# Soft-capped attention, gated MLP and gated convolution on one core: earlier loads of weight pieces and last values, and a third key tile added on VectorE for six head pairs

## The chip, the cores and the metric

The kernel runs on one core of one Trainium2 chip, in a single launch. The metric is the device time of that core in microseconds (us). The kernel before takes 324.7 us, the median of three runs (323.39, 324.70 and 325.33). One execution was profiled; it took 323.47 us, of which 321.3 us lie between its first and its last instruction.

## The reference, cut to what matters

Three stages run one after the other on 2 batches of 448 positions. The change touches the first alone.

```python
# 1. attention, 2 batches x 12 heads, 448 positions, head size 64
scores = (q @ k.T) / sqrt(64)
scores = cap * tanh(scores / cap)               # cap = 30
attn = softmax(scores)                          # exp, divided by (sum over keys + 1e-9)
x = concat_heads(attn @ v)                      # (2, 448, 768)
# 2. gated MLP, d_model 768, d_ff 1024
h = gelu(x @ w_in); u, v = halves of h
x = x + (u * (w_sg @ layernorm(v) * g_ln + b_sg)) @ w_out
# 3. gated convolution over the positions, three taps
h = relu(x @ w_in2); y = (h * sigmoid(conv(h))) @ w_out2
```

What the change computes otherwise is the sum over keys in the softmax: the terms are added in another place, and the sum is the same.

## The kernel before, in words

**Pairs, halves and rounds.** The 24 heads are worked in 12 pairs, numbered 0 to 11. The 448 keys of a head are cut in tiles of 128, 128, 128 and 64. A pair has two halves: half 0 holds the first two key tiles of both heads, half 1 the third tile and the last 64 keys. The loop in `attention` counts rounds R; in round R = 2N + half the function `scores` issues the products of queries and keys of pair N for that half. ScalarE applies tanh and exp to them in turn (`soft`, `expo`), and leaves exp(scores) in a tile `raw`. The scores of a half go to one PSUM tile `sc` that has one buffer, so the next half's scores wait until the tanh of this half has read it. I call rounds 2N and 2N+1 together "the stretch of pair N".

**Values and sums.** Two rounds later (`LAGS`), `values` multiplies exp(scores) by the values V into PSUM: half 0 first (key tiles 0 and 1), then half 1 (the last 64 keys, from the tile `vlast`, and key tile 2). So in the stretch of pair N TensorE issues the scores of pair N and the values of pair N-1. The sum over keys is taken by products with tiles of ones, in sets of four matmuls of 32 columns each. For half 0 VectorE first adds key tile 1 to key tile 0 (line 462; the result is `held[N]`, a tile named `sm`), and one set multiplies `sm` by ones. In half 1 one set multiplies key tile 2 of `raw` by ones and one set the last 64 keys. All TensorE instructions of this stage are chained in the order in which the code is written (`ordered`), so one that waits holds up all behind it.

**Normalising.** When a pair is done, ScalarE copies output and sums to `E` (line 532); a DMA from GpSimd's queue gathers the sums of two pairs into `ss` (line 534), VectorE takes the reciprocal (lines 552 and 553), a DMA writes it to `d` (line 556), four DMAs spread it over the partitions as `rb` (line 562), and VectorE multiplies (line 569) and splits the result in a high and a low part, `X`.

**Loads.** SyncE issues nearly all DMAs of this stage, and `sync` chains them in one order. `load(N+2)`, in round 2N, brings queries and keys (`qr`: two DMAs, `kr`: three); `load_v(N+1)` brings V; `load_vlast(n0, n1)` brings the last values of pairs n0 to n1-1 in four DMAs: pairs 0 to 2 at the start, pairs 3 to 11 in round 6. `prep_q` and `prep_k` split queries and keys on VectorE (lines 106 and 109) before the scores of that pair.

**Weight pieces.** The 12 pieces of the MLP's first weight, 512 KB each and stored as 64-bit numbers, are loaded into tiles `f` (named `f64` in the program; four buffers) in the rounds that the table `WIN` lists, and decoded in three steps that fall due 5, 6 and 7 ticks later; a round has two ticks. A decode is a cast to `hd` on VectorE (line 155; for later pieces on ScalarE, line 153), a shift-and-or (line 159), a cast to `WI` (line 165) and a subtraction (line 168). The first step is pinned behind the newest instructions noted in `lasta` and `lastv`:

```python
            with pin(lasta), pin(lastv):
                if top_eng == "a":
                    A.activation(half, top, AF.Copy)
                else:
                    V.tensor_copy(half, top)
```

The scheduler of the language sets the rest of VectorE's order by a simulated time, within such pins.

**Filling and the rest.** In rounds 15, 19 and 23 (`FILL`) TensorE also does six matmuls of the MLP; they need `X` and the first weight pieces. From about 108 us on the MLP and the convolution follow, with TensorE working without a gap. Lines 112 to 114 are their matmuls.

Of the kernel before, what the change touches and what calls it, by code (L numbers as in the profile page):

```python
# [23 lines left out]
NK = DM // P  # L24
# [13 lines left out]

TAKEN = 4

WARM = 10

K0 = 2 * P

IDLE = {0: (1, 4)}

WIN = (3, 5, 7, 9, 12, 15, 17, 19, 21, 22, 23, 24)
WOS = (0, 0, 1, 4, 4, 7, 7, 7, 10, 10, 11, 15)
W2I = (12, 12, 13, 13, 15, 17, 22, 24, 26, 30, 30, 33)
W2O = (0, 0, 1, 3, 4, 6, 7, 8, 8, 10, 10, 11, 11, 11, 11, 12, 13, 14, 15, 17, 18, 18, 19, 19)  # L50
# [3 lines left out]
def stages(  # L54
# [160 lines left out]
    def wi_piece(src, h, k):  # L215
        return WI[h], src, k, h * DH, (h + 1) * DH
# [66 lines left out]
    def attention(att, psa):  # L283
# [58 lines left out]
                for c in range(2):  # L342
                    sync(vlast[c * D : (c + 1) * D, n0:n1, r], v[r, n0:n1, 3, r])

        load_vlast(0, 3)
        if WARM:

            wz = att.tile([P, S], F32R, tag="rb", name="wz", bufs=2)
# [37 lines left out]
        def scores(N, half, then=None):  # L386

            R = 2 * N + half
            q, K = Qt[N], Kt[N % 2]
            ps = psa.tile([P, 4, 512], F32, tag="sc", name="sc", bufs=1)  # L390
            raw = raws[N, half] = att.tile([P, 4, S], F32, tag="raw", name="raw", bufs=3)

            sc = qreg if N else qscale

            def soft(x, ps):
                with pin(lasta):
                    lasta[0] = A.activation(x, ps, AF.Tanh, scale=sc)  # L397
                if N == 1 and half:
                    with pin(lasta):
                        late.pop()()  # L400
                if half or N:
                    expo(x)

            def expo(x):
                with pin(lasta):
                    lasta[0] = A.activation(x, x, AF.Exp, scale=creg)  # L406

            if half:
                ps = ps.rearrange("p (h a) c -> p h (a c)", h=2)[:, :, : 3 * 288]
                ps = ps.rearrange("p h (i c) -> p h i c", i=3)[:, :, :, :HS]  # L410
                raw = raws[N, half] = raw[:, :3].rearrange("p t s -> p (t s)").rearrange(
                    "p (h i c) -> p h i c", h=2, i=3
                )

            for g in range(2 * half, 2 * half + 2):
                to = ps
                if R == 0 and g == 0:
                    to = sums.rearrange("p (t c) -> p t c", t=3)
                c = slice(g * P, (g + 1) * P)
                if g < 2:  # L420

                    for i, (j, l) in enumerate(((0, 0), (0, 1), (1, 0))):
                        for h in range(2):
                            r = slice(h * D, (h + 1) * D)
                            ordered(to[:, g * 2 + h, :S], lhsT=K[r, j, c], rhs=q[r, l], start=i == 0, stop=i == 2)
                elif g == 2:
                    qr, kr = qraw[N]
                    x = qr.rearrange("p (i c) -> p i c", i=2)
                    for h in range(2):
                        r = slice(h * D, (h + 1) * D)  # L430
                        for i in range(2):
                            o, w = slice(i * D, (i + 1) * D), slice(K0 + i * D, K0 + (i + 1) * D)
                            ordered(ps[o, h, :2], lhsT=kr[r, w], rhs=x[r], start=True, stop=True)
                else:

                    qr, kr = qraw.pop(N)
                    for h in range(2):
                        r = slice(h * D, (h + 1) * D)
                        for i in range(2):
                            ordered(  # L440
                                ps[i * D : (i + 1) * D, h, 2], lhsT=kr[r, ST:],
                                rhs=qr[r, i * HS : (i + 1) * HS], start=True, stop=True,
                            )
                if N == 0 and g < 2:
                    soft(raw[:, 2 * g : 2 * g + 2], to[:, 2 * g : 2 * g + 2, :S])
                    if g:
                        expo(raw[:, 0:2])
                        expo(raw[:, 2:4])
                if R == 2 and g == 0:
                    set_guard()  # L450
                if R in IDLE and g == IDLE[R][0]:
                    for _ in range(IDLE[R][1]):
                        ordered(idle, lhsT=wz[:, :P], rhs=wz, start=True, stop=True)
            if then:
                then()
            if half:
                soft(raw, ps)
            elif N:
                soft(raw, ps[:, :, :S])
            if half == 0:  # L460
                held[N] = att.tile([P, 2, S], F32, tag="sm", name="sm", bufs=2)
                sms[N] = [V.tensor_tensor(out=held[N], in0=raw[:, 0:2], in1=raw[:, 2:4], op=ALU.add)]  # L462
# [27 lines left out]
        def values(N, half, done=False):  # L490
            if not done:
                if half == 0:
                    start_values(N)
                    value(N, 0)
                    value(N, 1)
                else:
                    value(N, 3)
                    value(N, 2)
            ps, su, both = acc[N]
            raw = raws.pop((N, half))  # L500

            for g in range(2 * half, 3 * half + 1):
                x = raw if half else held.pop(N)
                for t in range(4):
                    h, c = divmod(t, 2)
                    ordered(
                        su[t * 32 : (t + 1) * 32],
                        lhsT=ones[2 if g < 3 else c],
                        rhs=x[:, h, g - 2 + c if g == 2 else 2] if half else x[:, h, c * HS : (c + 1) * HS],
                        start=False, stop=g == 3, tile_position=(0, t * 32), skip_group_check=True,  # L510
                    )
            if half:
                del acc[N]
                norm(N, both)
# [94 lines left out]
        for R in range(2 * NN + LAGS[1] + 1):  # L609
            N, half = divmod(R, 2)  # L610
            if R == 23:
                columns(att)
            for j, at in enumerate(WIN):
                if at == R:
                    top_eng = "v" if R < 11 else "a"
                    wdec(*wi_piece(w_in, j // NK, j % NK), att, 4, hi_eng="v", wait=(5, 6, 7), top_eng=top_eng)
            if R < 2 * NN:
                if half == 0 and N + 2 < NN:
                    load(N + 2)
                if half == 0 and N + 1 < NN:  # L620
                    load_v(N + 1)
                if R == 6:
                    load_vlast(3, NN)
                if R == 1:

                    start_values(0)
                    scores(N, half)
                    value(0, 0)
                    value(0, 1)
                elif R == 3:  # L630

                    def sums0():
                        values(0, 1, True)
                        for _ in range(2):
                            ordered(idle, lhsT=wz[:, :P], rhs=wz, start=True, stop=True)

                    scores(N, half, sums0)
                    done += 1
                else:
                    scores(N, half)  # L640
                if R == 2:
                    values(0, 0, True)
                    value(0, 3)
                    value(0, 2)
                    done += 1
                if half == 0 and N + 1 < NN:
                    with pin(sms[N - 1]) if N else ExitStack():
                        prep_q(N + 1)
                        prep_k(N + 1)
            def units():  # L650

                i, k0, k1 = FILL[R]
                if k0 == 0:
                    if i == 1:
                        fill[-1] = psa.tile([P, 4, 512], F32, tag="sc", name="fi", bufs=1)
                    fill[i] = fill[-1][:, i, :S] if i % 2 else psm.tile([P, 512], F32, tag="mo", name="mo")[:, :S]
                for k in range(k0, k1):
                    mmw(fill[i], 0, i, k, ordered)
                if k1 == NK:
                    u_done(0, i, fill[i])  # L660
            if R in FILL and R >= 2 * NN:
                units()
            tick()
            if R > 2 and done < 2 * NN and R - done >= LAGS[R >= LAGS[2]]:
                values(*divmod(done, 2))
                done += 1
                if R == 2 * NN:
                    values(*divmod(done, 2))
                    done += 1
            if R in FILL and R < 2 * NN:  # L670
                units()
            tick()
# [428 lines left out]
```

## Time and profile before

| | |
|---|---|
| runs shown | 323.39, 324.70, 325.33 us; median 324.7 |
| profiled execution | 323.47 us, span 321.3 us |
| TensorE (PE) busy | 313.5 us, 98% of the span |
| VectorE (DVE) busy | 222.0 us, 69% |
| ScalarE (ACT) busy | 206.6 us, 64% |
| GpSimd (POOL) busy | 37.4 us, 12% |
| mean granted TensorE clock | 0.997 of full speed |
| DMA moved | 37.73 MB, 117 GB/s over the span |

Times in rows are us from the span's start. PE rows are matmuls and PEld rows weight loads, which run beside them; a 32-bit matmul that isn't in the fp32r form shows as two records, so a set of four with ones is eight records. In a timeline a row is one group of like instructions: its start, its length, engine, line, operation, what is written from what, the count, and in brackets how long the engine had been idle and what ended that. In a table of stretches the numbers behind the busy times (with counts of instructions) are the granted TensorE clock, the DMA share and GB/s. SPq is SyncE's queue: its time is that of issuing, not of moving data.

### The profile page before, as it was taken

What the parts mean: (1) busy time and instruction counts of PE and PEld (TensorE: products, weight loads), DVE (VectorE), ACT (ScalarE), POOL (GpSimd) and SP (SyncE); (2) the same over time, 40 slices, a digit from 0 to 9 for tenths busy, and PEclk for the clock granted to TensorE, in tenths of its full rate; (3) what the DMA queues carried; (4) which work ended last, traced back from release to release, by engine and by line L of the source; (5) the groups of instructions that cost most, each with busy time, mean ns of one, the idle gap of its engine ahead of it and who ended that gap; (6) DMA issues with size and microseconds to landing.
All of it is one profiled execution on the core that took longest, in us unless ns stands there. A gap on an engine that the chain in (4) does not pass through costs nothing.

```text
span 321.3 us, 6377 instructions
## 1 busy us (share of the span) xinstructions
PE 313.5 (98%) x2398; PEld 259.3 (81%) x2398; DVE 222.0 (69%) x460; ACT 206.6 (64%) x342; POOL 37.4 (12%) x75
## 2 busy tenths in 40 slices
PE   8999999999999999999999999999999999999993
PEld 6566656666677889988999999999999999999992
DVE  3458596698568879988996899979999998000000
ACT  4999989898973447746944754568886988111010
POOL 3000141441333020211112000000000000000000
PEclk9999999999999999999999999999999999999998
DMA  3478886857242153331134670021583201110111
GB/s 114 116 219 209 246 232 151 240 165 243 93 131 89 31 159 97 93 98 50 51 98 134 203 285 1 3 65 66 141 317 98 74 27 58 58 60 29 57 57 39
DMA packets 24528, 37.73 MB, mean 117 GB/s; under 512 B 7609, under 2 KB 22473, under 8 KB 24489
## 3 DMA queue, kind: packets, MB, share of 16 engines
q1 hardware_dynamic: 22552, 34.22, 35.1%
q0 software_dynamic: 1632, 2.61, 2.8%
q8 instruction: 21, 0.34, 0.5%
q10 hardware_dynamic: 304, 0.41, 0.4%
q14 instruction: 19, 0.15, 0.2%
HBM read 34.39 MB, written 2.79 MB: 116 GB/s over the span
## 4 chain that ended last, share of the span: by engine, by line
PE 81%; DMA 2%; DVE 0%; ACT 0%; SPq 0%; issue 0%; ACTq 0%
PE mo L113 18%; PE mo L112 18%; PE mo L114 18%; PE pv L380 8%; PE sc L380 4%; PE mo L795 3%; PE mo L797 3%; PE mo L796 3%; PE mo L380 3%; PE fi L380 2%; DMA ss<-E 1%; DMA kr<-in_kT_dram 1%; PE mo L841 1%; PE mo L842 1%; DVE sm L462 0%; ACT o L982 0%
## 5 line engine op out<-in xcount | busy, mean ns | idle before, releaser
L113 PE MATMUL mo<-X,WI 128*128 128x448 f32 x120 | 43.9, 366 | 0.0
L114 PE MATMUL mo<-X,WI 128*128 128x448 f32 x120 | 43.8, 365 | 0.0
L112 PE MATMUL mo<-X,WI 128*128 128x448 f32 x120 | 43.4, 365 | 0.0
L406 ACT ACTIVATE raw<-raw 128x1344 f32<-128x1344 f32 (+2 forms) x25 | 36.4, 1460 | 0.7
L397 ACT ACTIVATE raw<-sc 128x1792 f32<-128x1792 f32 (+1 forms) x22 | 32.4, 1474 | 4.4 <-PE sc L380 4.4
L112 PE MATMUL mo<-HG,W 128*128 128x448 f32 x96 | 34.4, 365 | 0.0
L114 PE MATMUL mo<-HG,W 128*128 128x448 f32 x96 | 34.4, 365 | 0.0
L113 PE MATMUL mo<-HG,W 128*128 128x448 f32 x96 | 34.4, 365 | 0.0
L380 PE MATMUL pv<-raw,V 128*32 128x224 f32 x576 | 32.9, 357 | 0.0
L985 ACT ACTIVATE o<-mo 128x448 f32<-128x448 f32 x11 | 5.8, 540 | 34.9 <-PE mo L114 31.7
L380 PEld LDWEIGHTS pv<-raw,V 128*32 128x32 f32 x576 | 19.0, 109 | 11.5 <-issue 5.6
L113 PEld LDWEIGHTS mo<-X,WI 128*128 128x128 f32 x120 | 22.5, 188 | 1.9
L114 PEld LDWEIGHTS mo<-X,WI 128*128 128x128 f32 x120 | 22.5, 188 | 1.9
L112 PEld LDWEIGHTS mo<-X,WI 128*128 128x128 f32 x120 | 22.5, 188 | 1.9
L153 ACT ACTIVATE hs<-f 128x256 f16<-128x256 bf16 x36 | 16.6, 488 | 7.8 <-DMA f<-in_w_in_dram 4.8
L114 PEld LDWEIGHTS mo<-HG,W 128*128 128x128 f32 x96 | 18.0, 188 | 1.4
L113 PEld LDWEIGHTS mo<-HG,W 128*128 128x128 f32 x96 | 18.0, 188 | 1.4
L112 PEld LDWEIGHTS mo<-HG,W 128*128 128x128 f32 x96 | 18.0, 188 | 1.4
L168 DVE TENSOR_TENSOR WI<-f,WI 128x256 fp32r<-128x256 f32 (+1 forms) x36 | 18.2, 509 | 1.0 <-ACT WI L163 0.7
L113 PE MATMUL mo<-gl,WO 128*128 128x448 f32 x48 | 17.4, 367 | 0.0
L114 PE MATMUL mo<-GH,WO 128*128 128x448 f32 x48 | 17.2, 366 | 0.0
L380 PE MATMUL sc<-Q,K 64*128 64x448 f32 x138 | 17.2, 380 | 0.0
(156 smaller groups left out, 683.9 us busy)
## 6 DMA issues: line engine op xcount, KB each, us to landing
f<-in_w_out_dram SPq DMA_DIRECT2D x36, 255.8 KB, 2.9
f<-in_w_in_dram SPq DMA_DIRECT2D x12, 511.8 KB, 5.7
f<-in_w_in_dram SPq DMA_DIRECT2D x24, 255.8 KB, 3.4
qr<-in_qT_dram SPq DMA_DIRECT2D x23, 112.0 KB, 4.0
rb<-d POOLq DMA_DIRECT2D x22, 112.0 KB, 3.4
out_dram<-o SPq DMA_DIRECT2D x11, 224.0 KB, 2.1
V<-in_vL_dram SPq DMA_DIRECT2D x12, 192.0 KB, 4.7
kr<-in_kT_dram SPq DMA_DIRECT2D x11, 112.0 KB, 4.9
```

The costliest lines, as they stand in the source:

```text
L112: matmul(ps, lhsT=whi, rhs=xhi, start=start, stop=False)
L113: matmul(ps, lhsT=whi, rhs=xlo, start=False, stop=False)
L114: matmul(ps, lhsT=wlo, rhs=xhi, start=False, stop=stop)
L153: A.activation(half, top, AF.Copy)
L168: V.tensor_tensor(out=lo, in0=f(low), in1=f(hi), op=ALU.subtract)
L380: lastm[0] = T.matmul(*args, **kw)
L397: lasta[0] = A.activation(x, ps, AF.Tanh, scale=sc)
L406: lasta[0] = A.activation(x, x, AF.Exp, scale=creg)
L795: T.matmul(ps, lhsT=xs(0, k), rhs=WI[1][:, 0, k], start=k == 0, stop=False)
L796: T.matmul(ps, lhsT=xs(0, k), rhs=WI[1][:, 1, k], start=False, stop=False)
L797: T.matmul(ps, lhsT=xs(1, k), rhs=WI[1][:, 0, k], start=False, stop=k == NK - 1)
L985: A.activation(o, ps, AF.Copy, scale=0.5)
```

## The change

It has three parts.

1. **The pieces are asked for sooner.** `WIN` moves the loads of the first nine pieces one or two rounds forward, and a new table `WAIT` makes up for it: the decode steps fall due as many ticks later, so each is written at the same tick as before.
2. **The last values come in four groups** of three pairs, in rounds 0, 4, 8 and 12 (`LAST`), instead of three pairs at the start and nine in round 6.
3. **In pairs 1, 2, 3, 5, 7 and 9 (`ADD`) VectorE also adds key tile 2 to the held sum.** The addition is noted in `lastv`, so later pinned instructions stand behind it. The set of products for half 0 goes, and the one that multiplied key tile 2 takes `held` instead. One set of four matmuls per pair is left out.

```diff
+ADD = (1, 2, 3, 5, 7, 9)
...
-WIN = (3, 5, 7, 9, 12, 15, 17, 19, 21, 22, 23, 24)
+WIN = (1, 3, 5, 7, 10, 13, 15, 17, 20, 22, 23, 24)
+
+WAIT = (9, 9, 9, 9, 9, 9, 9, 9, 7, 5, 5, 5)
+
+LAST = {0: (0, 3), 4: (3, 6), 8: (6, 9), 12: (9, 12)}
...
-        load_vlast(0, 3)
+        load_vlast(*LAST[0])
...
             if half:
                 soft(raw, ps)
+                if N in ADD:
+                    x = held[N].rearrange("p h (i c) -> p h i c", i=2)
+                    lastv[0] = V.tensor_tensor(out=x, in0=x, in1=raw[:, :, :2], op=ALU.add)
...
-            for g in range(2 * half, 3 * half + 1):
-                x = raw if half else held.pop(N)
+            for g in ((0, 3) if half else ()) if N in ADD else ((2, 3) if half else (0,)):
+                x = raw if g else held.pop(N)
...
-                        rhs=x[:, h, g - 2 + c if g == 2 else 2] if half else x[:, h, c * HS : (c + 1) * HS],
+                        rhs=x[:, h, c if g == 2 else 2] if g else x[:, h, c * HS : (c + 1) * HS],
...
-                    top_eng = "v" if R < 11 else "a"
-                    wdec(*wi_piece(w_in, j // NK, j % NK), att, 4, hi_eng="v", wait=(5, 6, 7), top_eng=top_eng)
+                    k, top_eng = WAIT[j], "v" if j < 4 else "a"
+                    wdec(
+                        *wi_piece(w_in, j // NK, j % NK), att, 4, hi_eng="v", wait=(k, k + 1, k + 2), top_eng=top_eng
+                    )
...
-                if R == 6:
-                    load_vlast(3, NN)
+                if R and R in LAST:
+                    load_vlast(*LAST[R])
```

**On TensorE**, in the stretch of pair 4, where the values of pair 3 are worked, before:

```order
L380 MATMUL sc_501<-Q_425,K0_87 128x448 x12
L380 MATMUL pv_157<-raw_408,V_311 32x224 x16
L380 MATMUL pv_157<-sm_423,ones2_144 32x224 x4
L380 MATMUL sc_557<-qr_304,kr_305 64x2x224 x4
L380 MATMUL sc_557<-qr_304,kr_305 64x224 x4
L380 MATMUL pv_157<-raw_456,vlast_108 64x224 x4
L380 MATMUL pv_157<-raw_456,V_311 32x224 x8
L380 MATMUL pv_157<-raw_456,ones2_144 32x224 x4
```

and now:

```order
L386 MATMUL sc_502<-Q_425,K0_87 128x448 x12
L386 MATMUL pv_157<-raw_408,V_314 32x224 x16
L386 MATMUL sc_552<-qr_307,kr_308 64x2x224 x4
L386 MATMUL sc_552<-qr_307,kr_308 64x224 x4
L386 MATMUL pv_157<-raw_452,vlast_108 64x224 x4
L386 MATMUL pv_157<-raw_452,V_314 32x224 x8
L386 MATMUL pv_157<-sm_423,ones2_144 32x224 x4
```

The set with `sm_423`, the held sum of pair 3, has moved behind the values of half 1, and the set with key tile 2 is gone.

**On VectorE**, from the split of pair 5's keys (`K1_88<-kr_395`) to the held sum of pair 4 (`sm_517`), before. `ss` are the sums of pairs 0 and 1, and `f64_453` is the third weight piece:

```order
L109 TENSOR_TENSOR K1_88<-kr_395,K1_88 128x256
L552 TENSOR_SCALAR ss_297<-ss_297,one_72 128x14
L155 CAST hd0_135<-f64_453 128x512
L553 RECIPROCAL ss_297<-ss_297 128x14
L159 SCALAR_TENSOR_TENSOR f64_453<-f64_453,hd0_135 128x512
L165 CAST WI0_76<-f64_453 128x512
L168 TENSOR_TENSOR WI0_76<-f64_453,WI0_76 128x512
L462 TENSOR_TENSOR sm_517<-raw_502 128x896
```

and now (`f64_278` is the second piece, `f64_359` the third, and `sm_518` the held sum of pair 4):

```order
L115 TENSOR_TENSOR K1_88<-kr_399,K1_88 128x256
L561 TENSOR_SCALAR ss_299<-ss_299,one_72 128x14
L161 CAST hd0_135<-f64_359 128x512
L562 RECIPROCAL ss_299<-ss_299 128x14
L165 SCALAR_TENSOR_TENSOR f64_359<-f64_359,hd0_135 128x512
L171 CAST WI0_76<-f64_359 128x512
L174 TENSOR_TENSOR WI0_76<-f64_359,WI0_76 128x512
L466 TENSOR_TENSOR sm_423<-sm_423,raw_452 128x896
L161 CAST hd1_136<-f64_278 128x512
L165 SCALAR_TENSOR_TENSOR f64_278<-f64_278,hd1_136 128x512
L171 CAST WI0_76<-f64_278 128x512
L471 TENSOR_TENSOR sm_518<-raw_503 128x896
```

The new addition for pair 3 stands behind the split of pair 5's keys, the sums of pairs 0 and 1 and a whole decode, and a second decode follows it ahead of pair 4's sum. (The last two rows have one subtraction into `WI0_76` between them, like the one shown.) Before, the second piece was decoded a pair earlier, in front of pair 3's sum.

**In SyncE's queue**, from V of pair 3 to the keys of pair 5, before (the names `qr_394` and `kr_395` are pair 5's):

```order
L86 DMA V_311<-in_vL_dram 128x384
L86 DMA f64_356<-in_w_in_dram 128x2047
L86 DMA qr_394<-in_qT_dram 64x448 x2
L86 DMA kr_395<-in_kT_dram 64x448
L86 DMA kr_395<-in_kT_dram 64x384
L86 DMA kr_395<-in_kT_dram 64x64
```

and now (`kr_399` is pair 5's):

```order
L92 DMA V_314<-in_vL_dram 128x384
L92 DMA vlast_108<-in_vL_dram 64x3x64 x4
L92 DMA f64_359<-in_w_in_dram 128x2047
L92 DMA qr_398<-in_qT_dram 64x448 x2
L92 DMA kr_399<-in_kT_dram 64x448
L92 DMA kr_399<-in_kT_dram 64x384
L92 DMA kr_399<-in_kT_dram 64x64
```

Four loads of last values have come in ahead of pair 5's queries and keys; the piece in this place is now the third instead of the second, which has moved up by a pair, as the first has.

## Rows read from the trace of the kernel before

**Rows 1.** The page: span, busy time and share of each engine.

```profile
span 321.3 us, 6377 instructions
...
PE 313.5 (98%) x2398; PEld 259.3 (81%) x2398; DVE 222.0 (69%) x460; ACT 206.6 (64%) x342; POOL 37.4 (12%) x75
```

**Rows 2.** Stretches of pairs 3, 4, 5, 7, and rest: length, PE, PEld, DVE, ACT, POOL busy.

```profile
24.53:31.37 6.84, 6.84 (x113) 4.40 (x109) 5.46 (x11) 6.62 (x6) 0.62 (x1) 1.00 0.92 222
31.37:38.22 6.85, 6.85 (x113) 4.39 (x110) 3.21 (x7) 6.62 (x6) 0.00 (x0) 1.00 0.87 214
38.22:45.78 7.56, 7.04 (x113) 4.19 (x110) 6.62 (x13) 6.58 (x6) 2.42 (x4) 1.00 0.86 255
...
52.61:61.35 8.74, 8.45 (x119) 5.26 (x115) 8.06 (x17) 8.48 (x8) 3.95 (x7) 1.00 0.79 208
...
108.20:316.00 207.80, 207.80 (x1008) 188.78 (x1006) 149.42 (x317) 116.89 (x259) 10.38 (x15) 1.00 0.29 93
```

**Rows 3.** Timeline of ScalarE in the stretch of pair 3.

```profile
26.06 1.66 ACT L397 ACTIVATE raw<-sc 128x1792 f32<-128x1792 f32 x1 [0.16 <-PE sc L380]
...
32.89 1.67 ACT L397 ACTIVATE raw<-sc 128x1792 f32<-128x1792 f32 x1 [0.17 <-PE sc L380]
```

**Rows 4.** Waits of TensorE's matmuls, those for VectorE's sums: total, times, longest.

```profile
PE pv L380 <- DVE sm L462: 0.8, 2, 0.5
```

**Rows 5.** Timeline of VectorE from 33 us on.

```profile
33.31 0.28 DVE L106 CAST K<-kr 128x256 fp32r<-128x256 f32 x1
...
34.38 0.23 DVE L552 TENSOR_SCALAR ss<-ss,one 128x14 f32<-128x14 f32 x1
38.44 0.47 DVE L155 CAST hd<-f 128x512 f16<-128x512 bf16 x1 [3.83 <-DMA f<-in_w_in_dram]
...
40.78 1.08 DVE L462 TENSOR_TENSOR sm<-raw 128x896 f32<-128x896 f32 x1
```

**Rows 6.** Timeline of VectorE before the held sum of pair 6.

```profile
51.70 0.23 DVE L552 TENSOR_SCALAR ss<-ss,one 128x14 f32<-128x14 f32 x1 [2.80 <-DMA ss<-E]
```

**Rows 7.** Timeline of TensorE in the stretch of pair 3.

```profile
25.96 1.76 PE L380 MATMUL pv<-raw,V 128*32 128x224 f32 x32
27.50 0.60 PE L380 MATMUL pv<-sm,ones 128*32 128x224 f32 x8
28.03 1.36 PE L380 MATMUL sc<-qr,kr 64*64 64x448 f32 x16
...
30.48 0.96 PE L380 MATMUL pv<-raw,ones 128*32 128x224 f32 x16
31.37 1.49 PE L380 MATMUL sc<-Q,K 64*128 64x448 f32 x12
```

**Rows 8.** Timeline of SyncE's queue: start and length of issuing.

```profile
7.73 2.62 SPq L86 DMA_DIRECT2D vlast<-in_vL_dram  x4
...
24.55 0.43 SPq L86 DMA_DIRECT2D f<-in_w_in_dram  x1
25.09 1.11 SPq L86 DMA_DIRECT2D qr<-in_qT_dram  x2
26.30 1.83 SPq L86 DMA_DIRECT2D kr<-in_kT_dram  x3
```

**Rows 9.** DMA issues from 15.2 to 16.4 us: count, KB each, us to landing.

```profile
qr<-in_qT_dram SPq DMA_DIRECT2D x2, 112.0 KB, 2.6
```

**Rows 10.** DMA issues between 26.3 and 28.2 us.

```profile
kr<-in_kT_dram SPq DMA_DIRECT2D x1, 96.0 KB, 4.6
```

**Rows 11.** Timeline of VectorE at the split of pair 3's keys.

```profile
19.74 0.29 DVE L106 CAST K<-kr 128x256 fp32r<-128x256 f32 x1 [0.86 <-DMA kr<-in_kT_dram]
```

**Rows 12.** Stretches at the end of the span: granted clock is the third number from the right.

```profile
318.00:319.00 1.00, 0.00 (x0) 0.00 (x0) 0.00 (x0) 0.00 (x0) 0.00 (x0) 1.00 0.33 112
...
320.00:321.40 1.40, 0.00 (x0) 0.00 (x0) 0.00 (x0) 0.00 (x0) 0.00 (x0) 0.50 0.02 6
```

**Rows 13.** DMA issues between 18.9 and 19.5 us.

```profile
f<-in_w_in_dram SPq DMA_DIRECT2D x1, 511.8 KB, 4.1
```

## The prediction

> **What bounds the kernel now.** I read the busy shares first. TensorE is busy for 98% of the span, VectorE for 69% and ScalarE for 64% [rows 1]. Then the same by stretch, because the shares are means over stages. From 108 us to 316 us TensorE is busy for all of 207.8 us [rows 2]: what happens before only moves this block, and a microsecond won or lost in attention is one at the end. In attention the stretch of a plain pair takes 6.85 us, with TensorE never idle and ScalarE busy for 6.62 us of it [rows 2]. Two engines are close to the limit there, so I read a stretch of each. From one wide tanh to the next ScalarE takes 32.89 - 26.06 = 6.83 us, and 0.17 us of that is a wait for TensorE's scores [rows 3]. So ScalarE could repeat in 6.66 us, and no faster.
>
> Last the waits. TensorE's matmuls wait for VectorE's held sums twice, 0.8 us in all [rows 4]. One wait is in the stretch of pair 5, which takes 7.56 us instead of 6.85, so 0.52 us idle cost 0.71 us [rows 2]. The other is in the stretch of pair 7: 8.74 us, 8.45 busy [rows 2]; by the same ratio its 0.29 us cost 0.40. The reader is to see why the sums were late. At 38.44 us VectorE had stood for 3.83 us at a piece's first cast until its DMA landed, and the held sum behind it began only at 40.78 [rows 5]. At 51.70 it had stood for 2.80 us until the sums `ss` of pairs 2 and 3 had come [rows 6]; their DMA stood in GpSimd's queue behind one that needed the reciprocal, which in turn stood behind that cast.
>
> **The change part by part.** *Pieces sooner.* The third piece is asked for one load of queries and keys sooner, and the second and third decode fall behind later work on VectorE. The 3.83 us wait goes, the reciprocal comes sooner, and with it the DMAs of the sums. Both waits of TensorE go: -0.71 - 0.40 = -1.11 us.
>
> *One set less in six pairs.* Forty records, 32 of values and 8 of a set, take TensorE from 25.96 to 28.03 us [rows 7], so a set is 2.07 x 8/40 = 0.41 us, and six are 2.5 us. But with 0.41 us less TensorE is ahead of ScalarE, whose tanh must free the one `sc` buffer, and only the 0.17 us are left to win. I count them in the stretches of pairs 2, 3, 4 and 6, where the sums of pairs 1, 2, 3 and 5 are taken: -0.68 us at most. In those of pairs 8 and 10 ScalarE also casts a piece, so I count nothing (bounds: 0 and -0.17 each).
>
> *Six additions.* Each is like the held sum, 1.08 us [rows 5], and VectorE has the time: in the stretch of pair 4 it is busy for 3.21 us [rows 2]. What counts is where it stands. TensorE now needs the addition for the set it takes in the same pair's half 1, with the next pair's scores queued behind it. The addition for pair 3 stands behind the split of pair 5's keys, the sums `ss`, a decode and the reciprocal. So I work out when pair 5's keys land.
>
> *SyncE's queue.* Before, the 96 KB part of these keys was the second of three DMAs from 26.30 us, so issued at 26.9 [rows 8]. Now one more piece and four loads of last values go first. A piece takes 25.09 - 24.55 = 0.54 us of issuing, and four loads of 48 KB took 2.62 [rows 8]: 3.16 us together, and the part is issued at 30.1. How long it then takes to land no row shows for this order. The bounds are 2.6 us, as for queries in an emptier queue [rows 9], and 4.6, as for these keys in a full one [rows 10]. A piece and four loads lie right ahead of it, so I take 3.8, nearer to the full one: landed at 33.9 us.
>
> *The wait this makes.* From the cast of the keys to `ss` are 34.38 - 33.31 = 1.07 us, `ss` takes some 0.2, decode with reciprocal 40.78 - 38.44 = 2.34, the addition 1.08 [rows 5]: 4.7 us, and it is done at 38.6. TensorE wants it where the first set with `raw` stood, 30.48 - 24.53 = 5.95 us into a stretch (24.53 is 6.84 before 31.37) [rows 7]. Pair 4's stretch began at 31.37, so 37.3, and some 0.6 sooner, because TensorE is by then ahead by the first 0.34 of the 0.68 and leaves out the first set: 36.7. It waits 1.9 us. After it come two sets, 31.37 - 30.48 = 0.9 [rows 7], so pair 5 begins at 39.5 instead of 38.22: 1.3 us late.
>
> *The addition for pair 1.* The first piece now goes ahead of pair 3's queries and keys, which VectorE was already waiting for: 0.86 us at 19.74 [rows 11]. It delays them by at least its 0.54 us of issuing, and at most by 512 KB at the 214 GB/s of a full stretch [rows 2], 2.4 us. With 1.07 for the split and 1.08 for the addition, this one is done between 22.4 and 24.3 us. TensorE wants it at 17.7 + 5.95 = 23.6: a wait of 0 to 0.7 us. I put no price on it, since pair 5's start hangs on the landing of its keys and takes up what TensorE lost before.
>
> *Last values in four groups.* None is late: each group is asked for a pair or more ahead. Their price is the 2.62 us above; the two later groups of four meet SyncE when nothing of VectorE's stands at a load.
>
> *Sum.* Pair 5 begins 1.3 us late. The waits that go after that point give 0.71 + 0.40, the set of pair 5 up to 0.17: 1.3 - 1.28 = 0.0, which I round up to +0.1 for the small waits behind a full VectorE. The profiled 323.47 us (span 321.3 and 2.2 around it) become 323.6. It lies 1.2 us under the median of the runs shown, so the median of 324.7 becomes 324.8. With the landing at its bounds the sum is +0.9 (4.6 us) and -1.1 (2.6 us).
>
> **The rivals.** *The loads are in time.* If the queue, relieved of nine pairs' last values in one go, lands pair 5's keys before 32 us, no addition is late, and 1.11 + 0.68 us are won: 322.9 us. For it: the DMA share in this stretch was 0.87 [rows 2], and moving pieces forward fills earlier idle time. Against it: the 3.16 us of issuing are fixed by the order, and even 2.6 us to land is 32.7. The Trainium skill (DMA: Bandwidth & Descriptors, Rules for kernel authors) says to issue a DMA early and wait for it late. By that rule this rival would be the forecast; the rows show a queue in which what is issued early holds up what stands behind it.
>
> *VectorE stays behind: slower.* Behind the addition for pair 3 come a second decode and pair 4's held sum: 38.6 + 2.34 + 1.08 = 42.0 us. TensorE wants it 27.50 - 24.53 = 2.97 us [rows 7] into a stretch that begins at 39.5: 42.5. The margin is 0.5 us. If the keys land after some 34.8 us, or the decodes take half a microsecond longer, sums of pairs 4 and 6 are late again. Then pair 5 begins 1.0 us later still and the 1.11 us are not won back: 0.1 + 1.0 + 1.1 = +2.2, or 326.9 us. For it: VectorE's load rises by 6 x 1.08 = 6.5 us, in front of sums TensorE needs. Against it: pair 4's stretch left VectorE free for over half of its length [rows 2].
>
> *The clock falls.* A wait of 1.9 us leaves TensorE without work as no wait of this trace does. At the end, with no matmul after some 316 us, the granted clock was still 1.00 (2.4 GHz) from 318 to 319 us and 0.50 (1.2 GHz) after 320 [rows 12]. If the wait let it fall, and half of a stretch ran at the lower level, 3.4 us would take 6.8: +3.5, or 328.3 us. The row speaks against it: two microseconds without a matmul left the clock where it was. The Trainium skill (TensorE: Matmul & The Clock Gate, Why this matters for your kernels) warns that an idle gap between bursts of matmuls puts the clock back to its lower level; by that rule this rival has its chance, and no run here shows it yet.
>
> *The change doesn't do what it says.* If the third piece still lands too late for its new place, the 1.11 us stay lost: +1.2, or 325.9 us. Against it: it is issued some 5 us sooner, and a piece landed 4.1 us after its issue [rows 13].
>
> **How the numbers follow.** The forecast, no change, gets 0.60; the loads in time 0.20; VectorE behind 0.14; the clock 0.03; no effect 0.03. A measurement of this kernel can tell about 0.5%, or 1.6 us, from no change. The forecast with its own range of -1.1 to +0.9 us lies within it, and so does +1.2: same 0.63. Faster is the first rival: 0.20. Slower are the second and third: 0.17. The predicted time is 324.8 us. The range reaches down to 322.7, past the centre of the first rival, and up to 326.8, to the second: half of each and the clock lie outside, some 0.2.
>
> **What would show it.** TensorE's waits for held sums in the stretches of pairs 5 and 7 are gone, and VectorE no longer stands at a piece. In their place TensorE waits for `sm` by the addition's line in the stretch of pair 4, 1 to 3 us, right after the values of half 1, and up to 0.7 us in that of pair 2. VectorE waits for `kr` ahead of the first. ScalarE has no idle time in the stretch of pair 3. From 108 us on nothing changes but the start. The forecast is wrong if the keys of pair 5 are split before 32.5 us, if TensorE waits again in the stretches of pairs 5 or 7, or if the stretches of pairs 8 to 11 change length.

## The result and the profile after

The change made the kernel slower by 0.8%: 326.19 us, the median of ten runs (325.79 to 327.68), beside 323.59 us for the kernel before, also of ten (322.86 to 325.33); the ratio is 1.0078, 95% interval 1.0062 to 1.0094. The profiled execution took 325.88 us, 2.41 more than that of before. The forecast was no change, 324.8 us, counted from a median of three runs (324.7); against the 323.59 us of ten, the miss is 2.5 us. The time lies inside the range that was given, and outside the 0.5% that the likeliest case allowed: one of the cases with a small chance happened as well. Ratios here and below leave out executions over 1.5% slower than the fastest of their kernel: one of the kernel before (328.11 us), and three of twelve each of no_pair35 and vlast_pool_late (327.2 to 329.2 us).

The page of the kernel after, its span and the busy time of each engine, answers to [rows 1]:

```profile
span 324.0 us, 6294 instructions
PE 314.2 (97%) x2350; PEld 261.1 (81%) x2350; DVE 226.1 (70%) x466; ACT 205.9 (64%) x342; POOL 37.9 (12%) x75
```

TensorE has 48 matmul records fewer and is busy for 0.7 us longer. That is the first sign of a lower clock. The table of stretches (columns as in [rows 2]: length, then PE, PEld, DVE, ACT and POOL, granted clock, DMA share, GB/s) shows where; its rows are pairs 3, 4, 5, 6 and 7, and the rest:

```profile
24.96:31.65 6.69, 6.66 (x105) 4.43 (x102) 5.86 (x10) 6.50 (x6) 0.62 (x1) 1.00 0.58 145
31.65:40.90 9.25, 6.85 (x104) 4.24 (x100) 5.94 (x13) 7.26 (x6) 0.66 (x2) 1.00 0.72 211
40.90:49.27 8.37, 8.37 (x112) 4.91 (x108) 4.86 (x9) 5.97 (x5) 3.50 (x6) 0.80 0.93 208
49.27:55.98 6.71, 6.63 (x104) 4.40 (x100) 5.78 (x13) 6.45 (x6) 1.20 (x2) 1.00 0.59 142
55.98:64.26 8.28, 8.28 (x119) 5.31 (x116) 7.44 (x15) 8.10 (x8) 2.92 (x5) 1.00 0.92 262
110.84:318.50 207.66, 207.66 (x1009) 189.13 (x1007) 148.54 (x314) 116.67 (x259) 10.38 (x15) 1.00 0.28 93
```

Beside before's, stretch by stretch, the differences in us add up to the 2.70 of the span:

| up to pair 1 | 1 and 2 | 3 | 4 | 5 | 6 | 7 | 8 | 9 | 10 | from pair 11 to the end |
|---|---|---|---|---|---|---|---|---|---|---|
| +0.45 | -0.02 | -0.15 | **+2.40** | **+0.81** | -0.12 | -0.46 | -0.15 | +0.02 | -0.14 | +0.06 |

Two stretches hold the loss. In that of pair 4 TensorE waits for the addition of pair 3. The waits of its matmuls for VectorE's sums (total, times, longest) are now one, where [rows 4] had two:

```profile
PE pv L386 <- DVE sm L466: 2.4, 1, 2.4
```

SyncE's queue ahead of pair 5's keys shows why [rows 8]: the four last values and the piece come first.

```profile
25.39 2.59 SPq L92 DMA_DIRECT2D vlast<-in_vL_dram  x4
28.02 0.60 SPq L92 DMA_DIRECT2D f<-in_w_in_dram  x1
28.73 1.13 SPq L92 DMA_DIRECT2D qr<-in_qT_dram  x2
29.95 1.82 SPq L92 DMA_DIRECT2D kr<-in_kT_dram  x3
```

The 96 KB part was issued at 30.54 us and took as long to land as in [rows 10] (DMA issues from 30.5 to 31.1 us: count, KB, us to landing):

```profile
kr<-in_kT_dram SPq DMA_DIRECT2D x1, 96.0 KB, 4.6
```

VectorE could therefore cast the keys at 35.25 us instead of 33.31 [rows 5], and the addition (line 466) stood at the end of the same chain as forecast:

```profile
35.25 0.29 DVE L112 CAST K<-kr 128x256 fp32r<-128x256 f32 x1 [1.10 <-DMA kr<-in_kT_dram]
36.33 0.23 DVE L561 TENSOR_SCALAR ss<-ss,one 128x14 f32<-128x14 f32 x1
38.87 1.08 DVE L466 TENSOR_TENSOR sm<-sm,raw 128x896 f32<-128x896 f32 x1
```

TensorE had nothing to do from the last values of pair 3 until then, and pair 5's scores queue behind (compare [rows 7]):

```profile
31.65 1.49 PE L386 MATMUL sc<-Q,K 64*128 64x448 f32 x12
36.66 0.98 PE L386 MATMUL pv<-raw,V 128*32 128x224 f32 x16
40.01 0.59 PE L386 MATMUL pv<-sm,ones 128*32 128x224 f32 x8 [2.36 <-DVE sm L466]
40.90 0.47 PE L386 MATMUL sc<-Q,K 64*128 64x448 f32 x2
```

The second loss is the clock. In stretches of 1 us, TensorE alone (length, busy, granted clock, DMA share, GB/s):

```profile
39.00:40.00 1.00, 0.00 (x0) 1.00 0.48 145
41.00:42.00 1.00, 1.00 (x8) 0.77 0.50 111
42.00:43.00 1.00, 1.00 (x10) 0.50 0.96 224
44.00:45.00 1.00, 1.00 (x16) 0.52 0.92 245
45.00:46.00 1.00, 1.00 (x27) 1.00 1.03 249
```

It was 1.00 (2.4 GHz) throughout the wait, fell to 0.50 (1.2 GHz) only after TensorE had resumed, and was back at 45 us. Pair 5's stretch should have lost its old wait, as pair 7's did; instead it took 8.37 us.

### The profile page after: what moved, and what is told of

The parts are those of the page before. It is cut to its first block, busy times and chain, and to the rows that moved or that the text cites. A ratio compares the mean times of both kernels' runs of the same rounds, so it can differ in the third digit from the quotient of the medians.

```text
span 324.0 us, 6294 instructions
## 1 busy us (share of the span) xinstructions
PE 314.2 (97%) x2350; PEld 261.1 (81%) x2350; DVE 226.1 (70%) x466; ACT 205.9 (64%) x342; POOL 37.9 (12%) x75
## 3 DMA queue, kind: packets, MB, share of 16 engines
q0 software_dynamic: 1632, 2.61, 3.0%
## 4 chain that ended last, share of the span: by engine, by line
PE 82%; SPq 6%; DMA 4%; ACT 3%; issue 2%; DVE 2%; DVEq 0%; ACTq 0%
PE mo L118 18%; PE mo L119 18%; PE mo L120 18%; PE pv L386 8%; SPq L92 6%; PE sc L386 5%; DMA kr<-in_kT_dram 4%; PE mo L808 3%; PE mo L807 3%; PE mo L806 3%; PE mo L386 2%; ACT raw L403 2%; PE fi L386 2%; PE mo L852 1%; PE mo L853 1%
## 5 line engine op out<-in xcount | busy, mean ns | idle before, releaser
L386 PE MATMUL pv<-raw,V 128*32 128x224 f32 x576 | 33.9, 366 | 0.0
L386 PE MATMUL sc<-Q,K 64*128 64x448 f32 x138 | 18.1, 395 | 0.0
L386 PE MATMUL sc<-qr,kr 64*64 64x448 f32 (+1 forms) x192 | 17.2, 454 | 0.7 <-ACT raw L403 0.2
```

The costliest lines, as they stand in the source:

```text
L386: lastm[0] = T.matmul(*args, **kw)
```

## The experiments

Twelve kernels ran in three sets, beside the kernel before, whose median was 324.18, 324.00 and 323.97 us. All start from the changed kernel. The table gives the ratio to the kernel before with its interval, two starts in the profiled execution (us), the wait for an addition with the pair that it belongs to, and whether the clock fell behind it.

| kernel | ratio | pair 5 begins | pair 8 begins | wait, pair | clock fell |
|---|---|---|---|---|---|
| before | | 38.22 | 61.35 | | |
| the change | 1.0078 [1.0062, 1.0094] | 40.90 | 64.26 | 2.36, 3 | yes |
| add_first | 1.0117 [1.0082, 1.0153] | 38.45 | 64.14 | 2.30, 5 | yes |
| no_pair3 | 1.0076 [1.0043, 1.0108] | 38.34 | 63.58 | 2.61, 5 | no |
| last_before | 0.9977 [0.9958, 0.9995] | 38.66 | 60.45 | none | no |
| keep_busy | 1.0058 [1.0032, 1.0084] | 41.49 | 63.98 | 0.64, 3 | no |
| split_even | 0.9978 [0.9957, 0.9999] | 38.17 | 60.28 | none | no |
| vlast_pool | 0.9986 [0.9968, 1.0004] | 39.03 | 60.87 | none | no |
| no_add | 1.0021 [0.9997, 1.0044] | 38.65 | 60.73 | none | no |
| add_alone | 1.0146 [1.0123, 1.0169] | 43.50 | 66.33 | 4.06, 3 | yes |
| round4_only | 1.0064 [1.0036, 1.0092] | 40.85 | 64.20 | 2.31, 3 | yes |
| round8_only | 1.0045 [1.0024, 1.0065] | 38.22 | 62.34 | 1.49, 5 | no |
| no_pair35 | 0.9994 [0.9961, 1.0027] | 38.41 | 61.31 | 0.4, 7 | no |
| vlast_pool_late | 1.0012 [0.9978, 1.0046] | 39.13 | 60.90 | 0.98, 3 | no |

**Is it the place of the one addition? (add_first, no_pair3)** My first theory was that pair 3's addition costs everything, because of where it stands on VectorE. Two kernels take it out of there, one by moving it ahead of pair 5's split, one by leaving it out.

```diff
-                    with pin(sms[N - 1]) if N else ExitStack():
+                    with pin(lastv) if N == 4 else pin(sms[N - 1]) if N else ExitStack():
                         prep_q(N + 1)
```

> The changed kernel, but the split of pair 5's queries and keys stands behind the addition for pair 3 on VectorE, instead of in front of it; nothing else is moved by hand, no load is touched. Theory 1 (place): the addition is late only because it stands behind keys that land at 35.2 us. Its input, the exp of pair 3's half 1, is ready at 32.4 us, so it is done by 33.6, in time that VectorE spent waiting for queries and keys. TensorE's wait of 2.4 us and the lower clock behind it go: pair 4's stretch 9.25 -> 6.7 us, pair 5's 8.37 -> 6.85, about 322.1 us for 326.2, so 0.995 of the kernel before. Pair 4's held sum then has hardly any margin (done about 41.3 us, wanted about 41.3), so up to 0.4 us may come back. Theory 2 (load): VectorE has 1.08 us of work too much in this stretch wherever it stands; the wait moves to pair 4's held sum, 1 us or more, about 324 to 325 us.

```diff
-ADD = (1, 2, 3, 5, 7, 9)
+ADD = (1, 2, 5, 7, 9)
```

> The changed kernel without the addition for pair 3 (five pairs add, pair 3 takes its two sets of products as before). Theory 1 (place): the one late addition and all that follows it go; the other five stand in time. Pair 4's stretch 9.25 -> 6.85 us, pair 5's 8.37 -> 6.85: about 322.3 us, 0.996 of the kernel before. Theory 2 (load, spread over all six additions): a sixth of the loss goes, about 325.5 us. Theory 3 (the clock falls on its own account in this stretch): the wait of 2.4 us goes but pair 5's stretch stays near 8.4 us, about 323.8.

Both expectations failed, and in the same way. Pair 5 began on time, and two pairs later TensorE stood still as long as before, now for pair 5's addition. TensorE, the DMA issues from 42.5 to 43.6 us, and VectorE of the kernel without pair 3's addition:

```profile
53.81 0.58 PE L386 MATMUL pv<-sm,ones 128*32 128x224 f32 x8 [2.61 <-DVE sm L466]
```

```profile
kr<-in_kT_dram SPq DMA_DIRECT2D x1, 96.0 KB, 7.3
```

```profile
50.03 0.29 DVE L112 CAST K<-kr 128x256 fp32r<-128x256 f32 x1 [0.91 <-DMA kr<-in_kT_dram]
52.67 1.08 DVE L466 TENSOR_TENSOR sm<-sm,raw 128x896 f32<-128x896 f32 x1
```

Pair 5's addition stands behind pair 7's keys as pair 3's does behind pair 5's, and the group of last values of round 8 stands ahead of pair 7's keys in SyncE's queue as that of round 4 does ahead of pair 5's. In the changed kernel this second wait is not seen, because TensorE is already 2.7 us late. So the theory of one place fell, and so did that of too much work on VectorE: no held sum of pair 4 was waited for. What was left is the queue.

**Is it the queue? (last_before, split_even, vlast_pool)** The first of these gives only the last values back to rounds 0 and 6; the second keeps four groups, two rounds later, where they stand ahead of the keys of even pairs; the third issues them from GpSimd.

```diff
-LAST = {0: (0, 3), 4: (3, 6), 8: (6, 9), 12: (9, 12)}
+LAST = {0: (0, 3), 6: (3, 12)}
```

> The changed kernel with the last values as before (three pairs at the start, nine in round 6): four DMAs of 2.6 us of issuing no longer stand ahead of pair 5's keys. Theory 1: the keys are issued at about 27.9 us, land at 31.5 to 32.5, the addition for pair 3 is done at about 37.3 and TensorE wants it at 37.6: no wait, or up to 0.5 us, clock at 1.00, 322.1 to 322.8 us. Rival (the keys' landing is set by the bytes ahead of them, not by SyncE's issuing): they still land at about 34.5, the wait shrinks to 1.7 us, and the time is 324 to 325.5.

```diff
+LAST = {0: (0, 3), 6: (3, 6), 10: (6, 9), 14: (9, 12)}
```

> The changed kernel with the same four groups of last values, but the later three asked for in rounds 6, 10 and 14 instead of 4, 8 and 12. In the queue they then stand ahead of the keys of pairs 6, 8 and 10 instead of 5, 7 and 9. The additions stand behind the splits of odd pairs' keys (3 behind 5, 5 behind 7), the pairs 4, 6 and 8 have none. Theory A (SyncE's issuing ahead of the keys that an addition stands behind): no wait of 2 us anywhere, pair 5's keys split at about 31 us, pair 7's at about 46, 322.8 to 323.4 us, 0.997 of the kernel before. Theory B (four groups cost more than two wherever they stand, since each takes 2.6 us of SyncE): a wait for the held sums of pairs 4, 6 or 8 or for their keys takes its place, 324.5 us or more.

```diff
-                    sync(vlast[c * D : (c + 1) * D, n0:n1, r], v[r, n0:n1, 3, r])
+                    if n0:
+                        with pin(lasta):
+                            G.dma_start(vlast[c * D : (c + 1) * D, n0:n1, r], v[r, n0:n1, 3, r])
+                    else:
+                        sync(vlast[c * D : (c + 1) * D, n0:n1, r], v[r, n0:n1, 3, r])
```

> The changed kernel with the last values of pairs 3 to 11 issued by GpSimd instead of SyncE: the same twelve DMAs, which GpSimd issues one after the other from about 3.5 us on, where it has nothing else to do. SyncE's queue holds only loads of queries, keys, V and pieces after the start. Theory A (SyncE's issuing is the cause): pair 5's keys land at 31.5 us, pair 7's at about 46, no wait for an addition, about 322.8 us. Rival (the bytes are the cause): the 576 KB now compete with the loads of the first pairs instead; pair 1 or 2 starts 1 to 2 us late and the time is 324 to 325.

All three lose the wait, and pair 8 begins 0.5 to 1.1 us sooner than before the change instead of 2.9 later. The two with SyncE alone are 0.2% faster than the kernel before, and 1% faster than the change. In the kernel with the last values as before, the stretches of pairs 4 and 6, the issuing of pair 5's keys in SyncE's queue, and their cast on VectorE:

```profile
31.66:38.66 7.00, 6.96 (x104) 4.58 (x100) 6.83 (x14) 6.81 (x6) 0.58 (x1) 1.00 0.97 234
...
45.48:52.17 6.69, 6.62 (x104) 4.40 (x100) 5.78 (x13) 6.45 (x6) 1.20 (x2) 1.00 0.68 198
```

```profile
26.72 1.82 SPq L92 DMA_DIRECT2D kr<-in_kT_dram  x3
```

```profile
31.29 0.30 DVE L112 CAST K<-kr 128x256 fp32r<-128x256 f32 x1
```

Pair 5's keys are split 4.0 us sooner than in the changed kernel: their issuing begins 3.2 us sooner (26.72 us for 29.95), 2.6 of it the four loads; the remaining 0.7 us, or more, is a shorter landing. With GpSimd, pair 1 began 0.7 us late beside the changed kernel (12.69 us for 11.98): the bytes then competed with the first loads, as its rival said, though it stayed ahead.

**Each place by itself (round4_only, round8_only)** keep one group ahead of an odd pair's keys each.

```diff
+LAST = {0: (0, 3), 4: (3, 6), 10: (6, 9), 14: (9, 12)}    # round4_only
+LAST = {0: (0, 3), 6: (3, 6), 8: (6, 9), 14: (9, 12)}     # round8_only
```

> The changed kernel with the last values asked for in rounds 0, 4, 10 and 14: one group stays ahead of pair 5's keys, none is ahead of pair 7's. Theory A (two places, each of which costs the whole; what pair 5 loses hides what pair 7 would lose): as the changed kernel: a wait of about 2.4 us for pair 3's addition, none for pair 5's, 325.5 to 326.5 us, 1.007 of the kernel before. Theory B (the losses of the two places add up): half of the loss goes, 324.5 to 325.

> The changed kernel with the last values asked for in rounds 0, 6, 8 and 14: pair 5's keys have no group of four loads ahead of them, pair 7's have one. Theory A (two places, each of which costs the whole): pair 5 begins at about 38.3 us, then TensorE waits some 2.5 us for pair 5's addition in the stretch of pair 6, 325.3 to 326.5 us. Theory B (pair 7's place costs little): as with rounds 6, 10 and 14, 323 to 324.

Either one alone brings most of the loss (1.0064 and 1.0045), and both together 1.0078. They don't add up: a delay at the first place covers the second. The profiled execution of round8_only took 324.23 us, 1.5 less than the median of its twelve (325.75), so its row in the table shows one of its shorter executions; the wait of 1.49 us, for some 2.5 expected, need not be that of the others.

**What the clock took (keep_busy).**

```diff
+            if half and N == 3:
+                for _ in range(11):
+                    ordered(idle, lhsT=Qt[4][:, 0, :P], rhs=Qt[4][:, 0], start=True, stop=True)
             for g in ((0, 3) if half else ()) if N in ADD else ((2, 3) if half else (0,)):
```

> The changed kernel with 11 matmuls of 448 columns on operands that nobody uses afterwards, put on TensorE right ahead of the set that waits for pair 3's addition: some 2.1 of the 2.4 us that it stood idle. The addition comes no sooner. If the idle time is what lowered the granted clock, pair 5 still begins at about 40.9 us, but its stretch runs at 1.00 and takes 6.9 us instead of 8.4: about 324.7 us. If the clock falls for another reason, pair 5's stretch stays near 8.4 us and the time at 326.2. If the matmuls take longer than the wait, pair 5 begins later by the surplus, up to 0.5 us.

TensorE in the wait, and the stretch of pair 5:

```profile
37.47 2.50 PE L386 MATMUL idle<-Q 128*128 128x448 f32 x11
40.60 0.59 PE L386 MATMUL pv<-sm,ones 128*32 128x224 f32 x8 [0.64 <-DVE sm L466]
```

```profile
41.49:48.33 6.84, 6.84 (x112) 4.38 (x108) 5.04 (x9) 5.96 (x5) 3.17 (x6) 1.00 0.97 209
```

With the wait filled the clock stays at 1.00 and the stretch takes 6.84 us instead of 8.37: the lower clock cost 1.53 us. Other executions agree: over ten of each, the mean granted clock was 0.994 to 1.000 (median 0.998) with the wait filled, and 0.985 to 0.997 (median 0.993) in the change. The time of the whole run gained little of it: 1.0058, which by the intervals is not clear of 1.0078. Pair 5 began 0.6 us later, because its queries happened to land later (their cast at 35.21 us for 33.75), and pair 7's stretch took 8.87 us for 8.28, with a new wait of 0.4 us for a held sum.

**The parts alone (no_add, add_alone, no_pair35).** The first leaves out all additions, the second loads pieces and last values as before, the third leaves out the additions of pairs 3 and 5.

```diff
+ADD = ()                                                  # no_add
+ADD = (1, 2, 7, 9)                                        # no_pair35
+WIN = (3, 5, 7, 9, 12, 15, 17, 19, 21, 22, 23, 24)        # add_alone
+WAIT = (5, 5, 5, 5, 5, 5, 5, 5, 5, 5, 5, 5)               # add_alone
+LAST = {0: (0, 3), 6: (3, 12)}                            # add_alone
```

> The changed kernel without any addition: pieces sooner and last values in four groups alone. Theory A: keys that land at 35 us for pair 5 and at 50 us for pair 7 are still split before TensorE wants them (38.2 and 52); only an addition behind them was late. TensorE's two waits of the kernel before go, so -0.7 to -1.1 us: about 322.6 to 323.0, ratio 0.997. Theory B (the late keys cost by themselves): pair 5 or pair 7 begins 1 us late or more, 324.5 to 326.

> The changed kernel with pieces and last values loaded as before: the six additions alone. Theory A (an addition costs what it stands behind): the addition for pair 3 now stands behind a decode whose piece lands at 38.4 us, so it is done at about 41.9 and TensorE wants it at 37.3: a wait of 4 us or more, pair 5 begins at about 42.5 us, and the clock may fall after it: 326.5 to 328.5 us, slower than the whole change. Theory B (the additions need no earlier pieces): as the kernel before or a little faster, 323 to 324.

> The changed kernel with four additions (pairs 1, 2, 7, 9); loads as changed. Theory A: both additions that stand behind late keys are gone, and no wait of 2 us is left: between the run without additions and the best ones, 323.5 to 324.3 us. Theory B (pair 7's addition, behind pair 9's keys and the group of round 12, is a third such place): a wait of 1 to 2.5 us in the stretch of pair 8, 325 to 326.

Without additions the late keys cost nothing: no wait of more than 0.3 us for a sum, pair 8 at 60.73. Its time was not the gain expected, though (1.0021); pair 11 begins 0.34 us sooner than before the change, and what follows took 1.2 us longer, 0.5 of it up to the last matmul, without a wait that the trace shows. Additions without the earlier pieces are worst of all, in TensorE's line

```profile
42.07 0.76 PE L386 MATMUL pv<-sm,ones 128*32 128x224 f32 x8 [4.06 <-DVE sm L466]
```

so the additions need the pieces to be early, and nothing may be put ahead of an odd pair's keys. The last values in four groups help in no run: the two fastest kernels have them as before, or in groups elsewhere. The run with four additions came out the same as before, with two shorter waits, of 0.81 us for pair 6's held sum and of 0.44 us for pair 7's addition, which hints at a third, weaker place.

**A try for more (vlast_pool_late)** issues the last values from GpSimd later.

```diff
-LAST = {0: (0, 3), 4: (3, 6), 8: (6, 9), 12: (9, 12)}
+LAST = {0: (0, 3), 4: (3, 6), 6: (6, 12)}
...
+                        with pin(lastg):
+                            lastg[0] = G.dma_start(vlast[c * D : (c + 1) * D, n0:n1, r], v[r, n0:n1, 3, r])
...
-                G.dma_start(ss[j * P // m : (j + 1) * P // m], e[::32, u : u + HS])
+                lastg[0] = G.dma_start(ss[j * P // m : (j + 1) * P // m], e[::32, u : u + HS])
```

> The changed kernel with the last values of pairs 3 to 5 and of pairs 6 to 11 issued by GpSimd, behind its gathers of the sums of pair 0 (19 us) and pair 1 (27 us): off SyncE, and not among the loads of the start. Theory A: as GpSimd issuing them at the start, but pair 1 no longer begins 0.9 us late and no V is waited for: 322.3 to 323.2 us, the fastest of all. Rival: on GpSimd they delay the DMAs of the sums, and what is won at pair 1 is lost in pairs 6 to 8: 323.5 to 324.5.

Neither came: 1.0012. Pair 1 began on time (11.57 us), but pair 4's keys were cast at 27.49 us instead of 25.42 in split_even, and VectorE's whole chain behind them, pair 3's addition at its end, ran late. SyncE issued these keys only 0.3 us later than there (from 21.87 us, for 21.56), with four loads from GpSimd, issued from 19.27 us on, under way beside them; the landing took longer. Here the bytes did what the issuing did elsewhere. The Trainium skill (DMA: Bandwidth & Descriptors, Issuing engines are not separate DMA queues) says that DMAs of all engines run on the same 16 DMA engines, and that issuing from another engine saves only issuing time. This run agrees. The page adds that this time is usually small beside the DMA itself; in this queue the 2.59 us of four loads decided.

## Why the prediction was right or wrong

**Which wait ends last: right.** The wait for pair 3's addition, behind pair 5's keys, in place of the two waits of before, was named with its place and its cause. VectorE's chain from the keys' cast to the end of the addition took 4.70 us (35.25 to 39.95), for 4.7. For pair 1's addition TensorE did not wait (0 to 0.7 us forecast).

**Its size: short.** The step that failed is the landing, "so I take 3.8, nearer to the full one". It was 4.6 us, the upper bound, from an issue 0.4 us later than worked out (30.54 for 30.1), which is no more than the later start of pair 3 (24.96 for 24.53). The addition was done at 39.95 instead of 38.6, and pair 5's beginning moved by 2.23 us against before (the stretches of pairs 1 to 4), not 1.3. With the upper bound the sum was +0.9. TensorE's lead of 0.6 us was not there either: ScalarE holds it to 6.7 us a stretch [rows 3], and it wanted the addition at 37.6.

**The clock: wrong, and the largest error.** "The row speaks against it" was a misreading of [rows 12]. That row shows a clock that stays high for a while after the last matmul and falls afterwards; it doesn't show that a gap is harmless. The same happened here, with TensorE busy again when it fell. Without the 1.53 us that keep_busy isolates, the +2.25 worked out below would be +0.72, near that +0.9. The rival had 0.03, at a price of +3.5 that was too high: it took half of a stretch's work to double, 3.4 us, where keep_busy shows 1.53. (Its 328.3 us also counts 0.1 twice.) The Trainium skill (TensorE: Matmul & The Clock Gate, Why this matters for your kernels) warns of idle gaps between bursts of matmuls, but of longer ones than the 1.9 us to which the prediction applied it. Of the four waits here behind which the clock fell, only that of 4.06 us in add_alone is one that its warning covers; the others were of 2.30 to 2.36 us, and the measurement decides.

**The two waits of before: right.** Pair 7's stretch lost 0.46 us (0.40 forecast), and pair 5's, at a clock of 1.00, takes 6.84 us in keep_busy, for 7.56 [rows 2]: 0.72 (0.71).

**A set less: right in size, too narrow in place.** Pairs 3, 6, 8 and 10 gained 0.12 to 0.15 each (0.17 at most was forecast, and nothing for 8 and 10); pair 2 gained nothing.

**The last values in four groups: wrong.** "The two later groups of four meet SyncE when nothing of VectorE's stands at a load" fails for round 8: pair 7's keys are late by the same mechanism, and only the first delay hid it. round8_only, no_pair3 and add_first show it.

**The sum.** 2.23 for pair 5's start, 0.81 for its stretch (1.53 - 0.72), and -0.79 for the rest (-0.12 - 0.46 - 0.15 + 0.02 - 0.14 + 0.06) are +2.25 us; the other 0.45 us of the span came before pair 1, whose start lay between 11.53 and 11.98 us in all kernels but vlast_pool, so I count it as scatter. "No change" had been +0.1. Of the rivals, the third (the clock) happened on top of the forecast; VectorE did not stay behind, since no held sum of pair 4 or 6 was late. (In no_pair3, keep_busy, round8_only and no_pair35 TensorE did wait for that of pair 6, for 0.4 to 0.8 us.) That the time lies inside the range is in part luck: its top, 326.8 us, was set by that second rival, which did not happen, and the clock was left outside.

**What stays open.** From the end of the last matmul to the end of the span the profiled executions took 5.1 to 6.3 us, in no order that follows the changes; it blurs gains of under 1 us, such as those of split_even and no_add.

## What to carry to other kernels

In a queue that issues in order, a load moved forward delays all that stand behind it: write down which of those the next pinned instruction needs, by issuing time and by landing. When a work item is made later than its consumer allows, look for the same pattern one period on before fixing it: here a second place two pairs later cost as much, and the first hid it. And where a forecast adds a wait of 2 us to TensorE, price the clock behind it as part of the wait.

## What I had not expected of the hardware

- The clock fell after waits of 2.36, 2.31, 2.30 and 4.06 us, but stayed at 1.00 after one of 2.61 (no_pair3). The first full stretch of 1 us after TensorE resumed there (at 53.81 us), and the same one in add_first, where it resumed at 53.65 us:

```profile
54.00:55.00 1.00, 1.00 (x18) 1.00 0.33 67
```

```profile
54.00:55.00 1.00, 1.00 (x16) 0.50 0.38 70
```

  So the length of a wait alone did not decide in these runs. Nor did the fall always come after TensorE had resumed: in add_first the mean from 53 to 54 us is 0.61, which is too low for a fall at 53.65 (0.82), so there it fell within the wait. What decides stays open.
- Four DMAs took SyncE 2.59 us with 48 KB each, and 2.67 us with 144 KB each (last_before, from 29.21 us). In the kernel before, the latter took 3.81 us (from 28.80 us). The three later groups took 2.59, 2.77 and 2.59 us, so they cost SyncE two to three times the issuing of the one that they replaced.
- The same 96 KB of keys took 4.6 us to land for pair 5 and 7.3 us for pair 7 (no_pair3).
